# A two-layer attention and SwiGLU kernel: moving small SBUF tiles ahead of the large ones, with fillers

## The chip, the cores and the metric

The kernel runs on one core of a Trainium2 chip. The metric is device time in microseconds of one execution. The core has five engines that run their own instruction streams and wait for each other through semaphores: PE (matrix products), DVE (vector), ACT (activations), POOL (GpSimd) and SP, which here only issues DMAs. SBUF is the on-chip memory of 128 partitions from which PE reads both of its operands; PSUM is where PE writes.

## The reference

Two identical rounds of attention with one key and value head (16 query heads of 28, 2048 tokens, width 448), each followed by a SwiGLU feed-forward of width 1792, all in float32.

```python
def _A_ref(x, wq, wk, wv, wo):
    q = (x @ wq).reshape(B, S, H, Dh).transpose(0, 2, 1, 3)
    k = x @ wk
    v = x @ wv
    scores = jnp.einsum("bhqd,bkd->bhqk", q, k) * (Dh ** -0.5)
    p = _softmax(scores, axis=-1)
    o = jnp.einsum("bhqk,bkd->bhqd", p, v)
    return o.transpose(0, 2, 1, 3).reshape(B, S, H * Dh) @ wo

def _B_ref(x, w_gate, w_up, w_down):
    return (_silu(x @ w_gate) * (x @ w_up)) @ w_down

x = x + _A_ref(_layernorm(x), ...)   # and
x = x + _B_ref(_layernorm(x), ...)   # both twice
```

## The kernel before

**Precision.** Most products are made of three matmuls in the type float32r, which takes one column of the moving operand per clock: each operand is split into a rounded high part and the rest (`xh` and `xl`, `wgh` and `wgl`, `wdh` and `wdl`, `woh` and `wol`, `onh` and `onl`; the two halves of `keys`, of `qstack` and of `h2`), and high × high, high × low and low × high are summed in PSUM. Only P·V is in plain float32, which the compiler runs as two halves per matmul.

**Stages.** The rows of x stay in SBUF as `xres`, 16 tiles of 128 rows by 448. A layer first projects queries, keys and values (function `product_T`, L315, 512 columns per matmul), and sends the queries through DRAM into three buffers `qstack0` to `qstack2`, which stand for 16 steps of four heads. Attention then runs 128 cycles per layer (`cycle`, two key tiles each). One cycle computes scores for two key tiles, 2 × 12 matmuls at L643: four heads lie in four strips of 32 partitions, so four matmuls run side by side, and three such steps make up the precise product. ACT takes the exponent of three heads from PSUM (L669, tile `pt`), DVE copies the fourth head to SBUF (L666, tile `pair`) and ACT takes its exponent there (L671). P·V of the cycle before (L703) follows the scores on PE. At certain cycles the output projection with `wo` is put in (`half_rows`, L631 and `full_rows`, L622).

The feed-forward takes 14 blocks of 128 hidden columns in groups of two, and four blocks of 512 rows each; one such unit is 42 matmuls of 512 columns for gate and up and 24 of 448 columns for the down product. They are written out by `side_by_side` (L335) in two lists, one for the lower 64 partitions and one for the upper 64, that run next to each other. ACT, DVE and POOL form silu(g) · u, split it (`h2`, whose low half DVE writes at L1041) and add the down product to `xres`. A few units run on the whole array (`product_T` again, and `by_tile`, L898).

**Order.** Every engine's order is the order in which the code is written (`manual_schedule`); the code places work into cycles by tables of numbers. Tiles come from pools. A pool places a tile, when it is first asked for, behind the tiles that it has, each rounded up to 32 bytes; a name that is asked for again goes to one of its `bufs` places, in turn. Pools lie behind one another; `ow` fills from the other end of SBUF. So where a tile starts follows from the order and the sizes of what was asked for before it. With `reuse_waits="tile"` a tile waits for the earlier tiles on whose bytes it lies.

The pool `pers` begins at a multiple of 256 bytes (`xres` is its first tile). The small tiles after `xres` shift everything behind it. These are the starts of the tiles that PE reads, in bytes past a multiple of 256:

| tiles | before | after |
|---|---|---|
| `xres` (read by DVE and POOL) | 0 | 0 |
| `keys`, `vsb`, `ident`, `xn` | 32 | 0 |
| `qstack`, `xh`, `xl`, `xd`, `wh`, `wl`, `wgh`, `wgl`, `wdh`, `wdl`, `pt`, `pair`, `q2` | 64 | 0 |
| `h2`, `woh`, `wol`, `onh`, `onl` | 224 | 0 |
| `kdiag` | 192 | 0 |

Rows inside these tiles are 512, 1792 or 2048 bytes long, all multiples of 256 (of `vsb` 128), so every slice that a matmul reads starts at the same offset as its tile (in `vsb` also 128 more).

The program also holds a second, slower version of the whole computation (`full` is true), which is entered only where a check on the softmax sums fails; it isn't executed here.

Of the kernel before, what the change touches and what calls it, by code (L numbers as in the profile page):

```python
# [8 lines left out]
F32 = mybir.dt.float32  # L9
F32R = mybir.dt.float32r  # L10
# [5 lines left out]
P = 128  # L16
S = 2048
D = 448
# [4 lines left out]
NT = S // P  # L23
# [13 lines left out]
@with_exitstack  # L37
def kernel(ctx: ExitStack, tc: tile.TileContext, *aps):

    nc = tc.nc
    keep = ctx.enter_context(tc.tile_pool(name="keep", bufs=1))
    fine = keep.tile([P, 16], F32, name="fine")
    nc.gpsimd.memset(fine, 1.0)
    least = keep.tile([P, 1], F32, name="least")
    whole = keep.tile([1, 1], F32, name="whole")
    forward(tc, (fine, least, whole), False, *aps)
    ok = nc.values_load(whole[0:1, 0:1].bitcast(mybir.dt.int32), skip_runtime_bounds_check_because="compared with 0 only")  # L50
    with tc.If(ok == 0, label="again"):
        forward(tc, None, True, *aps)
# [3 lines left out]
def forward(  # L56
# [24 lines left out]
    pers = ctx.enter_context(tc.tile_pool(name="pers", bufs=1))  # L81
# [52 lines left out]
    def split(hi, lo, raw):  # L134
        nc.gpsimd.tensor_scalar(hi, raw, 1.0, 0.0, ALU.mult, ALU.add)
        nc.gpsimd.tensor_tensor(lo, raw, hi, ALU.subtract)

    xres = pers.tile([P, NT, D], F32, name="xres")
    stats = pers.tile([P, NT, 6], F32, name="stats")
    mv = pers.tile([P, NT, 2], F32, name="mv")  # L140
    halfn = pers.tile([P, 4], F32, name="halfn")
    ident = pers.tile([P, P], F32, name="ident")
    vsb = pers.tile([P, NT, 32], F32, name="vsb")
    keys = [pers.tile([P, 2, 512], F32R, name=f"keys{c}") for c in range(NC)]
    warm = pers.tile([P, 1], F32, name="warm")
    qts = [pers.tile([P, 2, 512], F32R, name=f"qstack{n}") for n in range(3)]
    qraw = pers.tile([P, 512], F32, name="qraw")
    bottom = pers.tile([4, 32], F32, name="bottom")
    kd, mask = None, None
    if not full:  # L150
        kd, mask = pers.tile([P, 4, P], F32R, name="kdiag"), pers.tile([P, 16, 4], F32, name="mask")

    def weights(fc):
        fs = slice(P * fc, P * fc + P)
# [175 lines left out]
    def side_by_side(lower, upper):  # L330

        assert len(lower) == len(upper)
        for two in zip(lower, upper):
            for po, (a, b), start, stop in two:
                nc.tensor.matmul(po, a, b, start=start, stop=stop, skip_group_check=True)  # L335

    seen = pers.tile([P, 4], F32, name="seen")

    def between(*pos):

# [5 lines left out]
    class Attention:  # L346
# [229 lines left out]
        def scores(self, ff, xb):  # L576
            next(switch)
            inner = ExitStack()
            with tc.tile_pool(name=f"ow{self.layer}", bufs=1, side="right", reuse_waits="tile") as ow:
# [72 lines left out]
                bufs = [wp.tile([P, 3, 512], F32, name=f"pt{y}") for y in range(4)]  # L652
# [66 lines left out]
                def post(i):  # L719

                    c, g = GR[i]
                    out2 = accs.pop(i)
                    oraw, rb = out2[:, 0, :], out2[:, 1, :]
                    rs = ow.tile([P, 16], F32, name="rs", bufs=2)
                    nc.sync.dma_start(rs, oraw[DH::32, :].rearrange("j (p n) -> j p n", n=16))

                    def rest():
                        if fine is not None:
                            under = ow.tile([P, 16], F32, name="under", bufs=2)
                            for bound, op in ((LIMIT, ALU.is_lt), (1.0 / LIMIT, ALU.is_gt)):  # L730
                                nc.vector.tensor_scalar(under, rs, bound, None, op)
                                nc.vector.tensor_tensor(fine, fine, under, ALU.mult)
                        nc.vector.reciprocal(rs, rs)
                        rd = dram.tile([4, 512], F32, name="rd", bufs=2)
                        nc.sync.dma_start(rd.rearrange("j (p n) -> (j p) n", n=16), rs)
                        nc.sync.dma_start(rb, rd[:, None, :].to_broadcast([4, 32, 512]))
                        if g == 0:
                            on[c] = (
                                ow.tile([P, NG, 512], F32R, name="onh"),
                                ow.tile([P, NG, 512], F32R, name="onl"),  # L740
                            )
                        nc.gpsimd.tensor_tensor(rb, oraw, rb, ALU.mult)

                    def spread():
                        if g == 0:
                            moved[c] = dram.tile([2 * DH, 512], F32, name=f"moved{self.layer}_{c}")
                            for q in (0, 1):
                                nc.sync.dma_start(moved[c][DH * q : DH * q + DH, :], rb[64 + 32 * q : 64 + 32 * q + DH, :])
                            for q in (0, 1):
                                n0 = 2 * DH - 8 + 4 * q  # L750
                                nc.sync.dma_start(rb[32 * q + DH : 32 * q + 32, :], moved[c][n0 : n0 + 4, :])
                            nc.sync.dma_start(rb[64:128, :], rb[0:64, :])
                            return
                        n0 = 16 * g - 16
                        for q in range(4):
                            nc.sync.dma_start(rb[DH + q :: 32, :], moved[c][n0 + 4 * q : n0 + 4 * q + 4, :])

                    def parts():
                        oh, ol = on[c]
                        split(oh[:, g, :], ol[:, g, :], rb)  # L760
                        if g == NG - 1 and c < NC - 1:
                            todo.append(c)

                    return rest, spread, parts

                X0 = xtile(xpool)
# [441 lines left out]
```

## Time and profile before

| | us |
|---|---|
| median of 3 runs | 1944.67 (1944.64 to 1945.7) |
| the profiled execution | 1948.05 |
| its span | 1946.3 |
| PE busy | 1933.1 (99%) |
| ACT busy | 1256.8 (65%) |
| DVE busy | 978.1 (50%) |
| POOL busy | 563.8 (29%) |

How to read it. The rows of the page's part 5 name a line, an engine, an operation, the tile written and the tiles read, then the shape and the count; behind the bar stand the busy time in us, the mean duration of one in ns, and the idle time of the engine just before these instructions with what ended it. PEld is PE's weight load, which runs beside matmuls. A matmul's duration includes the way through the array, so matmuls overlap in the records, and a busy PE may still be slower than it could be. The pace, from the start of one matmul to the start of the next, is read from the timeline, whose rows begin with a start time in us and a duration in us, and merge neighbours of one kind (x3: three of them). Rows of a table of windows begin with the window and its length, then busy time and count for each engine, then the granted clock of PE, the share of the DMA engines and GB/s. Line numbers are those of the kernel before; in the kernel after, lines behind the top of `forward` are 11 higher.

### The profile page before, as it was taken

How to read it: one execution, taken by the hardware profiler on the slowest of the kernel's cores; microseconds unless marked ns; L12 is line 12 of the kernel's file. 1: busy time of each engine (PE TensorE's matmuls, PEld its weight loads, DVE VectorE, ACT ScalarE, POOL GpSimd, SP SyncE). 2: the span in 40 equal slices, each digit the busy share in tenths (PEclk: the TensorE clock that was granted, in tenths of full speed). 3: DMA queues.
4: the chain of work that ended last, by engine and by line, in shares of the span. 5: the costliest groups of instructions: out<-in, count | busy, mean ns of one | idle time of the engine just before them, and what ended most of it. 6: DMA issues, size and time to landing. Idle time of an engine off the chain costs nothing. (4 is left out here: it accounts for less than half of the span.)

```text
span 1946.3 us, 43775 instructions
## 1 busy us (share of the span) xinstructions
PE 1933.1 (99%) x18369; PEld 1325.7 (68%) x18369; DVE 978.1 (50%) x1675; ACT 1256.8 (65%) x1863; POOL 563.8 (29%) x608
## 2 busy tenths in 40 slices
PE   9999999999999999999999999999999999999998
PEld 7544544445469999999974445454454799988887
DVE  6655575665754322322665565657656532232223
ACT  4799899898953333333359998989989433333332
POOL 4213123122215333432342221122231352333420
PEclk9999999999999999999999999999999999999999
DMA  5211011021122011100251110110211220011102
GB/s 160 63 33 33 20 32 50 23 54 33 35 81 73 17 33 32 32 19 25 60 156 48 34 34 18 43 38 26 53 52 30 81 61 26 17 32 32 33 2 77
DMA packets 105474, 87.52 MB, mean 45 GB/s; under 512 B 25304, under 2 KB 85464, under 8 KB 105272
## 3 DMA queue, kind: packets, MB, share of 16 engines
q1 hardware_dynamic: 103576, 83.25, 15.4%
q8 instruction: 144, 2.36, 0.5%
q10 hardware_dynamic: 1696, 1.43, 0.2%
q14 instruction: 58, 0.48, 0.1%
HBM read 59.48 MB, written 23.33 MB: 43 GB/s over the span
## 5 line engine op out<-in xcount | busy, mean ns | idle before, releaser
L669 ACT ACTIVATE pt<-three 128x1536 f32<-128x1536 f32 x512 | 722.1, 1478 | 52.9 <-PE three L643 52.8
L703 PE MATMUL bank<-pt,vsb 128*32 128x512 f32 x3072 | 490.8, 598 | 0.6 <-ACT pt L669 0.6
L703 PE MATMUL bank<-pair,vsb 128*32 128x512 f32 x1024 | 487.7, 598 | 0.0
L643 PE MATMUL bank<-qstack,keys 32*128 32x512 f32 x1536 | 472.7, 425 | 0.0
L335 PE MATMUL bank<-xh,wgh 64*128 64x512 f32 x1712 | 439.0, 389 | 0.4 <-ACT seen L342 0.4
L643 PE MATMUL three<-qstack,keys 32*128 32x512 f32 x4608 | 429.0, 408 | 0.5 <-ACT stage L549 0.3
L643 PEld LDWEIGHTS bank<-qstack,keys 32*128 32x128 f32 x1536 | 243.2, 183 | 248.1 <-issue 125.4
L666 DVE COPY pair<-bank 128x512 f32<-128x512 f32 x512 | 353.9, 691 | 96.5 <-PE bank L643 65.6
L335 PE MATMUL bank<-xh,wgl 64*128 64x512 f32 x1391 | 363.8, 390 | 0.0
L335 PE MATMUL bank<-xl,wgh 64*128 64x512 f32 x1284 | 329.5, 389 | 0.0
L1035 DVE TENSOR_TENSOR sg<-bank,sg 128x512 f32<-128x512 f32 x112 | 77.3, 690 | 486.8 <-ACT sg L1034 476.3
L335 PE MATMUL bank<-wdh,h 64*128 64x448 f32 x1728 | 320.8, 363 | 0.8 <-DVE h L1041 0.4
L671 ACT ACTIVATE pair<-pair 128x1024 f32<-128x1024 f32 x254 | 277.6, 1093 | 0.0
L643 PEld LDWEIGHTS three<-qstack,keys 32*128 32x128 f32 x4608 | 262.0, 183 | 14.2 <-DVE xres L614 1.5
L703 PEld LDWEIGHTS bank<-pt,vsb 128*32 128x32 f32 x3072 | 101.7, 109 | 249.2 <-issue 153.2
L335 PEld LDWEIGHTS bank<-xh,wgh 64*128 64x128 f32 x1712 | 260.9, 184 | 15.2 <-issue 1.0
L915 POOL TENSOR_TENSOR xres<-stage,xres 128x448 f32<-128x448 f32 x107 | 126.1, 1197 | 479.9 <-ACT stage L914 479.7
L711 DVE TENSOR_TENSOR o<-bank,o 128x512 f32<-128x512 f32 x224 | 154.7, 691 | 202.1 <-PE bank L703 202.0
L335 PEld LDWEIGHTS bank<-wdh,h 64*128 64x128 f32 x1728 | 238.4, 184 | 12.4 <-DVE h L1041 1.2
L342 ACT COPY seen<-bank 128x1 f32<-128x1 f32 x646 | 79.4, 163 | 244.7 <-PE bank L335 242.0
L335 PEld LDWEIGHTS bank<-xh,wgl 64*128 64x128 f32 x1391 | 214.9, 184 | 12.6
L335 PE MATMUL bank<-wdl,h 64*128 64x448 f32 x864 | 212.0, 366 | 0.0
(150 smaller groups left out, 2133.2 us busy)
## 6 DMA issues: line engine op xcount, KB each, us to landing
o<-rd SPq DMA_DIRECT2D x32, 256.0 KB
qraw<-qd SPq DMA_DIRECT2D x128, 56.0 KB
xt<-tb SPq DMA_DIRECT2D x32, 224.0 KB
wdr<-in_B_w_down_dram SPq DMA_DIRECT2D x28, 224.0 KB
xn<-xt SPq DMA_DIRECT2D x8, 768.0 KB
wr<-in_B_w_gate_dram SPq DMA_DIRECT2D x28, 192.0 KB
wr<-in_B_w_up_dram SPq DMA_DIRECT2D x28, 192.0 KB
qd<-stage SPq DMA_DIRECT2D x20, 224.0 KB
```

The costliest lines, as they stand in the source:

```text
L335: nc.tensor.matmul(po, a, b, start=start, stop=stop, skip_group_check=True)
L342: nc.scalar.copy(seen[:, i : i + 1], po[:, 0:1])
L643: nc.tensor.matmul(three[:, j, :] if j < 3 else one, k[js, kp, ks], q[js, part, :], start=(z == 0), stop=(z == 2), tile_position=(32 * j, 0),)
L666: copies.append(nc.vector.tensor_copy(pt1, one))
L669: es.append(nc.scalar.activation(pt, threes[y], AF.Exp, scale=SCALE))
L671: es.append(nc.scalar.activation(pair, pair, AF.Exp, scale=SCALE))
L703: nc.tensor.matmul(to[32 * j : 32 * j + 32, :], vsb[:, n % NT, :], pts[n][j], start=(y == 0), stop=(y == 1), skip_group_check=True,)
L711: f = nc.vector.tensor_tensor(accs[i][:, 0, :], to, accs[i][:, 0, :], ALU.add)
L915: nc.gpsimd.tensor_tensor(r, s, r, ALU.add)
L1035: nc.vector.tensor_tensor(in_order(sg, True), natural(pg[1], True), in_order(sg, True), ALU.mult)
```

## The change

The small tiles of the pool `pers` are asked for first, also those that used to be asked for only when they were first needed (`rstd`, `few`, `ng`, `two`, `flat`, `seen`); a filler `pad` of 112 floats brings the next tile to a multiple of 256 bytes. `xres` and the large tiles follow. In the pool `ow` a filler of 120 floats is asked for behind the pair `onh`, `onl`. The result for the tiles' starts is in the table above. Nothing is written to a filler, and the early calls write nothing: the later calls of the same names get the same places.

```diff
-    xres = pers.tile([P, NT, D], F32, name="xres")
     stats = pers.tile([P, NT, 6], F32, name="stats")
     mv = pers.tile([P, NT, 2], F32, name="mv")
+    ident = pers.tile([P, P], F32, name="ident")
     halfn = pers.tile([P, 4], F32, name="halfn")
-    ident = pers.tile([P, P], F32, name="ident")
+    warm = pers.tile([P, 1], F32, name="warm")
+    bottom = pers.tile([4, 32], F32, name="bottom")
+    seen = pers.tile([P, 4], F32, name="seen")
+    mask = None
+    if not full:
+        mask = pers.tile([P, 16, 4], F32, name="mask")
+        for _ in range(2):
+            pers.tile([P, 4], F32, name="rstd", bufs=2)
+        pers.tile([P, 8], F32, name="few")
+        pers.tile([P, 64], F32, name="ng")
+        pers.tile([P, 4, 2, 16], F32R, name="two")
+        pers.tile([P, P], F32, name="flat")
+        pers.tile([P, 112], F32, name="pad")
+    xres = pers.tile([P, NT, D], F32, name="xres")
     vsb = pers.tile([P, NT, 32], F32, name="vsb")
     keys = [pers.tile([P, 2, 512], F32R, name=f"keys{c}") for c in range(NC)]
-    warm = pers.tile([P, 1], F32, name="warm")
     qts = [pers.tile([P, 2, 512], F32R, name=f"qstack{n}") for n in range(3)]
     qraw = pers.tile([P, 512], F32, name="qraw")
-    bottom = pers.tile([4, 32], F32, name="bottom")
-    kd, mask = None, None
+    kd = None
     if not full:
-        kd, mask = pers.tile([P, 4, P], F32R, name="kdiag"), pers.tile([P, 16, 4], F32, name="mask")
+        kd = pers.tile([P, 4, P], F32R, name="kdiag")
...
-
-    seen = pers.tile([P, 4], F32, name="seen")
...
                                 ow.tile([P, NG, 512], F32R, name="onh"),
                                 ow.tile([P, NG, 512], F32R, name="onl"),
                             )
+                            if not full:
+                                ow.tile([P, 120], F32, name="pad")
```

The order of instructions on PE, ACT, POOL and SP is the same before and after, row by row. On DVE the instructions stand in the same order too, with other waits at one place of each layer: at the first transposes into the tile `tb3` (shown as tb), in the first group of the feed-forward. Before, in a row:

```order
L230 TENSOR_SCALAR xn<-xres,mv,rstd 128x448 [waits DVE_49,Pool_49]
L271 STREAM_TRANSPOSE tb_6629<-xn 128x14x32 [waits DMAHW2_49,DVE_49]
L271 STREAM_TRANSPOSE tb_6629<-xn 128x14x32 [waits DVE_49] x3
L1035 TENSOR_TENSOR sg<-bank_6453,sg 128x512 [waits Activation_49]
L911 TENSOR_TENSOR xres<-bank_6455,xres 128x448 [waits PE_49]
```

After, in a row:

```order
L241 TENSOR_SCALAR xn<-xres,mv,rstd 128x448 [waits DVE_49,Pool_49]
L282 STREAM_TRANSPOSE tb_6640<-xn 128x14x32 [waits DVE_49] x4
L1046 TENSOR_TENSOR sg<-bank_6464,sg 128x512 [waits Activation_49]
L922 TENSOR_TENSOR xres<-bank_6466,xres 128x448 [waits PE_49]
L1052 TENSOR_TENSOR h_6745<-sg,h_6745 128x512 [waits DMAHW6_49,DMAHW5_49,DMAHW7_49,DMAHW0_49,Activation_49]
```

`tb3` lay over the bytes of the tile `rs` of attention before and waited for the last DMA on them (DMAHW2); now it lies behind them, and that wait stands at a later DVE instruction, the first copy into `xl`.

## The prediction

> **What bounds the kernel now.** I read the page first, then the distance from one matmul's start to the next in the timeline, because a PE that is busy 99% of the span says only that matmuls overlap without a hole, not that they follow each other as fast as they can.
>
> ```profile
> span 1946.3 us, 43775 instructions
> PE 1933.1 (99%) x18369; PEld 1325.7 (68%) x18369; DVE 978.1 (50%) x1675; ACT 1256.8 (65%) x1863; POOL 563.8 (29%) x608
> L703 PE MATMUL bank<-pt,vsb 128*32 128x512 f32 x3072 | 490.8, 598 | 0.6 <-ACT pt L669 0.6
> L643 PE MATMUL three<-qstack,keys 32*128 32x512 f32 x4608 | 429.0, 408 | 0.5 <-ACT stage L549 0.3
> L335 PE MATMUL bank<-xh,wgh 64*128 64x512 f32 x1712 | 439.0, 389 | 0.4 <-ACT seen L342 0.4
> L335 PE MATMUL bank<-wdh,h 64*128 64x448 f32 x1728 | 320.8, 363 | 0.8 <-DVE h L1041 0.4
> L335 PE MATMUL bank<-wdl,h 64*128 64x448 f32 x864 | 212.0, 366 | 0.0
> ```
>
> PE waits for nothing in any large group (idle before: 0.0 to 0.8 us each). So the time is the number of matmul steps times the pace of a step, and nothing on another engine, queue or DMA can save time as long as it hides behind PE. The diff issues the same instructions in the same order (below). Its whole effect on PE must therefore come through the pace. Here are the paces, in settled stretches of matmuls with one matmul to a step. The first fence is 512 columns at a granted clock of 0.50 (start of the kernel), then 512 columns at 1.00, first and last of 34.
>
> ```profile
> 14.70:17.80 3.10, 3.10 (x9) 2.37 (x8) 3.00 (x8) 0.00 (x0) 1.67 (x6) 0.50 1.03 397
> 562.10:569.60 7.50, 7.50 (x34) 6.20 (x33) 3.18 (x9) 1.81 (x3) 0.00 (x0) 1.00 0.25 65
> ...
> 14.75 0.63 PE L315 MATMUL bank<-xh,wh 128*128 128x512 f32 x1
> ...
> 17.74 0.63 PE L315 MATMUL bank<-xh,wl 128*128 128x512 f32 x1
> ...
> 562.13 0.39 PE L315 MATMUL bank<-xh,wgl 128*128 128x512 f32 x1
> ...
> 569.61 0.40 PE L315 MATMUL bank<-xh,wgl 128*128 128x512 f32 x1
> ```
>
> At half clock seven steps take 2.99 us, 427 ns each: 1.2 columns per ns. At full clock the stream alone should take half, 213.5 ns. It takes 7.48 us / 33 = 226.7 ns: 13.2 ns too much, which at half clock is not there at all. The next rows are 448 columns (stream alone 186.7 ns): 24 matmuls whose moving tile is `woh`, then 24 whose moving tile is `wdh` or `wdl`, first and last of each.
>
> ```profile
> 1174.19 0.37 PE L622 MATMUL three<-wol,onh 128*128 128x448 f32 x1
> ...
> 1178.85 0.36 PE L622 MATMUL three<-woh,onh 128*128 128x448 f32 x1
> ...
> 1936.14 0.37 PE L898 MATMUL bank<-wdh,h 128*128 128x448 f32 x1
> ...
> 1940.86 0.37 PE L898 MATMUL bank<-wdh,h 128*128 128x448 f32 x1
> ```
>
> 4.66/23 = 202.6 ns and 4.72/23 = 205.2 ns: 15.9 and 18.5 ns over the stream. The two have the same shape, the same weight tile offset (224) and differ in where the moving operand starts: 224 and 64 bytes past a multiple of 256. Finally P·V, whose fp32 matmuls run as two halves at two clocks per column.
>
> ```profile
> 251.13 0.60 PE L703 MATMUL bank<-pt,vsb 128*32 128x512 f32 x3
> ...
> 251.56 0.60 PE L703 MATMUL bank<-pt,vsb 128*32 128x512 f32 x3
> ...
> 251.99 0.60 PE L703 MATMUL bank<-pt,vsb 128*32 128x512 f32 x3
> ```
>
> 0.43 us a step against 2 × 213.5 = 427: an excess of about 3 ns or less, with its moving tile at offset 64 as well. So the excess appears only where columns are taken at the full rate of one float per 1/2.4 ns. Something that delivers the moving operand can't keep up by 13 to 18 ns a step there, and is hidden when the array takes half as much.
>
> My reading: delivery is in blocks of 128 bytes (32 columns, 32/2.4 = 13.3 ns). 2048 bytes from offset 64 touch 17 blocks instead of 16, and 17 × 13.3 = 226.7, the measured pace to the tenth. 1792 bytes from 64 or 224 touch 15 instead of 14, 200.0 ns, plus 2.6 or 5.2 that this doesn't explain. The block is an inference from these four numbers; no operand at a multiple of 128 is streamed at full rate anywhere in this trace.
>
> **The change part by part.** Instructions: none added, none removed. The unused tiles allocate without being written. On PE, ACT, POOL and SP every instruction keeps its place; DVE loses two wait-only entries, because `tb3` no longer lies over the old `rs` tiles. The wait for those tiles' last DMA goes to the first copy of `xl`. Its price is nothing: the last DMA out of `rs` is issued at 1525.9 and the last transposes into `tb3` (named tb here) run until 1550.5, some 25 us later; the DMA had landed.
>
> ```profile
> L735 SPq DMA_DIRECT2D rd<-rs x32: 327/347/469, 109.2 to 1525.9; - x32
> ...
> L271 DVE STREAM_TRANSPOSE tb<-xn x32: 602/634/643, 276.8 to 1550.5; 128x448 f32<-128x448 f32 x32
> ```
>
> Transfers: rows in SBUF now start at multiples of 256. They may get shorter; all but the first load of x and the weights are hidden behind PE, and `xres`, which the start waits for, lay at a multiple of 256 already. Zero. ACT, DVE and POOL operands: hidden behind PE except in attention, below. Zero.
>
> Steps outside the score matmuls. These rows are the matmul counts (the second column with an x belongs to the weight loads) of L315, L441, L335, L622, L631 and L898, in this order.
>
> ```profile
> 0.00:1947.00 1947.00, 112.95 (x462) 87.30 (x462) 1.00 0.16 45
> 0.00:1947.00 1947.00, 8.99 (x32) 5.89 (x32) 1.00 0.16 45
> 0.00:1947.00 1947.00, 786.17 (x7086) 730.78 (x7086) 1.00 0.16 45
> 0.00:1947.00 1947.00, 60.52 (x288) 53.46 (x288) 1.00 0.16 45
> 0.00:1947.00 1947.00, 11.94 (x96) 8.46 (x96) 1.00 0.16 45
> 0.00:1947.00 1947.00, 10.34 (x48) 9.01 (x48) 1.00 0.16 45
> ```
>
> L335 and L631 run two halves of the array side by side, two matmuls to a step. Of L335's 7086, 1728 + 864 have 448 columns: 1296 steps; the other 4494 have 512: 2247 steps. 512 columns: 2247 + 462 + 32 = 2741 steps. 448 columns from offset 64: 1296 + 48 = 1344; from offset 224: 288 + 48 = 336; together 1680.
>
> A 512-column step saves its extra block, but keeps what P·V pays over its stream, about 2.5 ns: 226.7 − 216.0 = 10.7. Bounds: at best 13.2 (nothing over the stream); at worst a loss, from the slowest steps seen, the first ones after a change of clock or shape, 18.57 to 19.73 in the next rows, 5 steps of 232 ns: −5. I take 10.7, since P·V is the nearest row of a stream without the excess. A 448-column step saves one block, 13.3; bounds 18.5 (the whole excess) and, for a loss, the same −5.
>
> ```profile
> 18.57 0.39 PE L315 MATMUL bank<-xl,wh 128*128 128x512 f32 x1
> ...
> 19.73 0.39 PE L315 MATMUL bank<-xh,wh 128*128 128x512 f32 x1
> ```
>
> 2741 × 10.7 = 29.3 us and 1680 × 13.3 = 22.4 us.
>
> The Trainium skill, "TensorE: Matmul & The Clock Gate", section "Back-to-back issue gap", gives N/2.4 + 2.5 ns for a warm matmul: 215.8 and 189.2. The P·V rows and the half-clock rows agree with that page, the full-rate rows miss it by 11 to 16 ns. By it the two terms would be 29.9 and 26.0, an estimate.
>
> In the feed-forward part the faster PE must not run into DVE's `h`: it ends at 605.88 and its first reader starts at 606.56, 0.68 us later, while the 21 steps of the unit around it save at most 0.23. No stall follows.
>
> ```profile
> 605.19 0.69 DVE L1041 TENSOR_TENSOR h<-sg,h 128x512 fp32r<-128x512 f32 x1 [0.16 <-ACT h L1038]
> 606.56 0.55 PE L335 MATMUL bank<-wdh,h 64*128 64x448 f32 x2
> ```
>
> Attention: six score steps a cycle, 256 cycles (6144/24). PE could save 6 × 10.7 = 64 ns a cycle. ACT allows less. A usual cycle, then the quickest:
>
> ```profile
> 249.95 2.80 ACT L669 ACTIVATE pt<-three 128x1536 f32<-128x1536 f32 x2
> 252.63 1.07 ACT L671 ACTIVATE pair<-pair 128x1024 f32<-128x1024 f32 x1
> 253.59 2.79 ACT L669 ACTIVATE pt<-three 128x1536 f32<-128x1536 f32 x2
> ...
> 224.57 2.79 ACT L669 ACTIVATE pt<-three 128x1536 f32<-128x1536 f32 x2
> 227.23 1.08 ACT L671 ACTIVATE pair<-pair 128x1024 f32<-128x1024 f32 x1
> 228.18 2.81 ACT L669 ACTIVATE pt<-three 128x1536 f32<-128x1536 f32 x2
> ```
>
> ACT's cycle is 3.64 us and consists of its own work end to end (2.68 to the pair, 0.96 after it); the quickest is 2.66 + 0.95 = 3.61. I take 3.61 for ACT's own limit, from which it sets the pace, and count 0.03 × 256 = 7.7 us; without that limit it would be 16.4.
>
> Sum: 29.3 + 22.4 + 7.7 = 59.4 us. The profiled execution took 1948.05 us with a span of 1946.3, 3.4 above the median of 1944.67; taken off the median the time is **1885 us**.
>
> **Rivals.**
>
> *Only part of the excess depends on the start (18%).* For it: the two 448-column rows. 64 bytes past a block cost 18.5, 32 bytes short of one cost 15.9, so a price by bytes of the first broken block (64 and 32) fits: 2.6 ns per 32 bytes. Then a start at 0 saves 5.3 ns a step: 4421 × 5.3 = 23.4, and 7.7 in attention (6 × 5.3 = 32 ns still reaches ACT's limit): 1914 us. Against it: 17 blocks fit the 512 columns exactly.
>
> *The excess is a fixed start-up of every full-rate stream (15%, no measurable change).* For it: any fixed cost also vanishes at half clock, and no aligned row refutes it. Only the difference between the two 448-column rows is then up for change: 1344 × 2.6 = 3.5 us at most, 1941 to 1945 us. Against it: a fixed cost would not be 13.2, 15.9 and 18.5. Beside it stands the Trainium skill, "SBUF — State Buffer", section "Door 1: The DMA port swizzle", which speaks of lines of 16 bytes; every tile before starts at a multiple of 32, so by that page nothing is misaligned and nothing changes. No run here shows a 16-byte line.
>
> *Equal starts collide (15%, slower).* After the change the moving stream, the next weights and ACT's writes all start at the same place of a 256-byte row; before, `keys` lay at 32 against `qstack` at 64, `h` at 224 against `wdh` at 64. If a weight load then holds up the stream in every step, the price is that of the unsettled steps, 5 ns: 4421 × 5 = 22 us, and 6 × 5 × 256 = 8 in attention: about 1975 us. It decides from 1 ns a step (0.2% of the time). Against it: `xh` and `wgh` share offset 64 already and show the plain 226.7, and the pair with equal offsets (224 and 224) is the quicker of the 448-column rows.
>
> **How the numbers follow.** The block reading has 52% and gives 1885. Its low end takes the whole excess off: 2741 × 13.2 + 1344 × 18.5 + 336 × 15.9 + 7.7 = 74 us, 1870. The upper end takes in the partial case and the unchanged one: 1946. Left out are the slower case (15%) and small tails. A measurement of this kernel tells 0.2% (4 us) from no change: its runs lie within 1.1 us. Faster by more: 52 + 18 = 70%; within: 15%; slower: 15%.
>
> **What would show it.** Right: L315's settled 512-column steps at 216 ns, 448-column ones at 189 to 193; P·V unchanged at 0.43 us; attention's cycle near 3.60 us with PE now waiting for ACT. Wrong: 226.7 again (fixed cost), some 221 (partial), or over 227 (collision). A cycle near 3.57 would say that ACT's limit was mine, not the chip's; a wait of PE for `h` or for weights would show cover gone that I counted on.

## The result and the profile after

The changed kernel takes 1937.50 us (median of 7 runs, 1936.91 to 1939.11) against 1944.67 us for the kernel before (7 runs, 1943.50 to 1945.70): a ratio of 0.9963 with a 95% interval of 0.9954 to 0.9972. It is faster, by 0.37% or 7.2 us, and not by the 59 us forecast.

The page after, its first lines and the groups that answer to those shown of before:

```profile
span 1935.7 us, 43773 instructions
PE 1923.0 (99%) x18369; PEld 1325.8 (68%) x18369; DVE 979.0 (51%) x1675; ACT 1254.1 (65%) x1863; POOL 563.4 (29%) x608
L712 PE MATMUL bank<-pt,vsb 128*32 128x512 f32 x3072 | 490.8, 598 | 0.6 <-ACT pt L678 0.6
L652 PE MATMUL three<-qstack,keys 32*128 32x512 f32 x4608 | 428.8, 408 | 0.5 <-ACT stage L558 0.3
L346 PE MATMUL bank<-xh,wgh 64*128 64x512 f32 x1712 | 419.7, 390 | 0.0
L346 PE MATMUL bank<-wdh,h 64*128 64x448 f32 x1728 | 313.2, 361 | 0.8 <-DVE h L1052 0.5
```

PE is still busy 99% of the span and still waits for nothing; score and P·V groups stand as they were, and only the feed-forward groups (L335 before, L346 now) shrank: 439.0 to 419.7 us and 320.8 to 313.2. By the starts of the first score matmul and the last P·V matmul of each layer, the span divides as follows (us):

| | start | attention 0 | feed-forward 0, projection 1 | attention 1 | feed-forward 1 |
|---|---|---|---|---|---|
| before | 65.9 | 493.2 | 468.1 | 493.4 | 425.5 |
| after | 63.6 | 492.6 | 464.4 | 492.8 | 422.2 |

The two feed-forward stretches give 7.0 us. The start holds the stretch at half clock, which differs from run to run (the whole start lasts 63.4 to 64.7 us in the profiles of the seven full kernels below, whatever the layout). The profiled execution of before lay 3.4 us above its median, that of after on it, so the 2.3 us of the start and the 1.2 us of attention in this table are not counted as the change's.

The pace, in the timeline after: 23 settled full-array steps of 512 columns, then two stretches of 35 matmuls with `woh` or `wol` as moving tile, then 24 with `wdh` or `wdl`, first and last of each:

```profile
561.64 0.39 PE L326 MATMUL bank<-xh,wgl 128*128 128x512 f32 x1
...
566.63 0.39 PE L326 MATMUL bank<-xh,wgl 128*128 128x512 f32 x1
...
1167.24 0.37 PE L631 MATMUL three<-wol,onh 128*128 128x448 f32 x1
...
1174.27 0.37 PE L631 MATMUL three<-woh,onl 128*128 128x448 f32 x1
...
1528.42 0.37 PE L631 MATMUL bank<-wol,onh 128*128 128x448 f32 x1
...
1535.31 0.37 PE L631 MATMUL bank<-woh,onl 128*128 128x448 f32 x1
...
1925.55 0.36 PE L909 MATMUL bank<-wdh,h 128*128 128x448 f32 x1
...
1930.21 0.37 PE L909 MATMUL bank<-wdh,h 128*128 128x448 f32 x1
```

512 columns: 4.99/22 = 226.8 ns, as before, though the moving tile now starts at a multiple of 256. 448 columns: 4.66/23 = 202.6 ns for `wdh` (205.2 before) and 7.03/34 = 206.8 in one stretch with `woh`, 6.89/34 = 202.6 in the other (202.6 before). The kernel has eight such stretches: before, all eight go at 202.5 to 202.8 ns; after, six do and two go at 206.7, with the same tiles. So not one of the three settled rows went where the forecast sent it, and `woh` shows two lasting paces in one layout.

Most matmuls stand in the two-lane part, which repeats a round of 33 steps: 11 of 512 columns, 6 of 448, 10 of 512, 6 of 448. Here is the same place of a round, five rounds apart, before and then after (the first `wdl` step of the shorter half):

```profile
701.63 0.54 PE L335 MATMUL bank<-wdl,h 64*128 64x448 f32 x2
...
738.09 0.54 PE L335 MATMUL bank<-wdl,h 64*128 64x448 f32 x2
```

```profile
701.31 0.50 PE L346 MATMUL bank<-wdl,h 64*128 64x448 f32 x2
...
737.44 0.50 PE L346 MATMUL bank<-wdl,h 64*128 64x448 f32 x2
```

36.46/5 = 7.292 us a round before, 36.13/5 = 7.226 after. The kernel has 2247/21 = 107 rounds, and 107 × 0.066 = 7.1 us: the whole gain. Counted over all matmul records of one lane, from one start to the next: a 448-column step followed by another takes 202.8 ns in place of 205.5 (1071 pairs, 2.9 us), the step from 512 to 448 columns 227.4 in place of 236.5 (214, 1.9 us), the step from 448 to 512 199.4 in place of 201.0 (209, 0.3 us), and 512 to 512 goes from 229.8 to 228.9 (2028, 1.8 us). What in the new layout did this was the question for the runs.

### The profile page after: what moved, and what is told of

The parts are those of the page before. It is cut to its first block, busy times and chain, and to the rows that moved or that the text cites. A ratio compares the mean times of both kernels' runs of the same rounds, so it can differ in the third digit from the quotient of the medians.

```text
span 1935.7 us, 43773 instructions
## 1 busy us (share of the span) xinstructions
PE 1923.0 (99%) x18369; PEld 1325.8 (68%) x18369; DVE 979.0 (51%) x1675; ACT 1254.1 (65%) x1863; POOL 563.4 (29%) x608
## 5 line engine op out<-in xcount | busy, mean ns | idle before, releaser
L678 ACT ACTIVATE pt<-three 128x1536 f32<-128x1536 f32 x512 | 733.4, 1523 | 52.5 <-PE three L652 52.5
L346 PE MATMUL bank<-xh,wgh 64*128 64x512 f32 x1712 | 419.7, 390 | 0.0
L346 PE MATMUL bank<-xh,wgl 64*128 64x512 f32 x1391 | 349.2, 388 | 0.0
L346 PE MATMUL bank<-wdh,h 64*128 64x448 f32 x1728 | 313.2, 361 | 0.8 <-DVE h L1052 0.5
L346 PE MATMUL bank<-xl,wgh 64*128 64x512 f32 x1284 | 312.4, 386 | 0.0
L680 ACT ACTIVATE pair<-pair 128x1024 f32<-128x1024 f32 x254 | 289.2, 1139 | 0.0
L346 PEld LDWEIGHTS bank<-xh,wgh 64*128 64x128 f32 x1712 | 241.6, 184 | 12.7 <-issue 1.0
L346 PEld LDWEIGHTS bank<-wdh,h 64*128 64x128 f32 x1728 | 225.2, 184 | 10.0 <-DVE h L1052 1.2
L346 PEld LDWEIGHTS bank<-xh,wgl 64*128 64x128 f32 x1391 | 200.8, 184 | 11.8
L1045 ACT ACTIVATE sg<-bank 128x512 f32<-128x512 f32 x112 | 66.9, 597 | 217.2 <-PE bank L346 212.9
```

The source lines that it names most:

```text
L678: es.append(nc.scalar.activation(pt, threes[y], AF.Exp, scale=SCALE))
L680: es.append(nc.scalar.activation(pair, pair, AF.Exp, scale=SCALE))
L1045: nc.scalar.activation(in_order(sg, True), natural(pg[0], True), AF.Silu)
```

## The experiments

The theories. *Block reading* (theory B, the forecast's own): the moving tile's start alone decides, in blocks of 128 bytes. *Multiples of 256* (theory A): the large tiles' own places count. *Fixed start-up* (theory F): neither. *Pairs* (called theory W, the weights' start, in the first series, and pair theory later): what counts is where the moving tile starts against the weight tile that is loaded while matmuls run; before, `h` as weights lay at 224 and `wdh` as moving tile at 64, and now both lie at 0.

### Series of matmuls with chosen starts

```diff
+        for i in range(32): mm(b[i % 4][:, 0:512], sta[:, 16 + 128 * (i % 4) : 144 + 128 * (i % 4)], mov[:, 0 + 512 * (i % 2) : 512 + 512 * (i % 2)], start=True, stop=True)  # N 512 mov 0 sta 64
...
```

> Leaves out the whole computation (the input is copied to the output) and runs series of 32 float32r matmuls, each series on a line of its own, with nothing to wait for; the moving tile's start, the weights' start and the number of columns change from series to series. Fixed start-up (theory F): the pace of 512 columns is 226 to 227 ns whatever the two starts are, of 448 columns 200 to 203 ns, and over all widths it is columns/2.4 ns plus a constant of 12 to 15 ns. Block reading (theory B, the one the forecast rests on): 213 to 216 ns at starts that are multiples of 128 bytes, 226 to 227 ns at the others, and the moving tile's start alone decides. Weights' start (theory W): 448 columns go at 202 to 203 ns where the weights start at the same offset from a multiple of 256 bytes as the moving tile or at 0, and at 205 to 206 ns where the weights start at 224 and the moving tile at 64, as it was in the kernel before; 512 columns do not change.

The timeline of PE has one row a series; the distance between two rows' starts, divided by 32, is the pace. Each series is shown with the row behind it: 512 columns with moving/weights starts 0/0 (L30) and 0/64 (L39); 448 columns with 0/0 (L48), 64/64 (L49), 224/224 (L50), 64/224 (L51), 0/224 (L52) and 64/0 (L53):

```profile
30.93 7.42 PE L30 MATMUL bank<-mov,sta 128*128 128x512 f32 x32
38.19 7.57 PE L31 MATMUL bank<-mov,sta 128*128 128x512 f32 x32
...
97.72 7.63 PE L39 MATMUL bank<-mov,sta 128*128 128x512 f32 x32
105.18 7.65 PE L40 MATMUL bank<-mov,sta 128*128 128x512 f32 x32
...
164.15 6.65 PE L48 MATMUL bank<-mov,sta 128*128 128x448 f32 x32
170.64 6.65 PE L49 MATMUL bank<-mov,sta 128*128 128x448 f32 x32
177.13 6.76 PE L50 MATMUL bank<-mov,sta 128*128 128x448 f32 x32
183.72 6.73 PE L51 MATMUL bank<-mov,sta 128*128 128x448 f32 x32
190.29 6.70 PE L52 MATMUL bank<-mov,sta 128*128 128x448 f32 x32
196.83 6.56 PE L53 MATMUL bank<-mov,sta 128*128 128x448 f32 x32
203.23 6.64 PE L54 MATMUL bank<-mov,sta 128*128 128x448 f32 x32
```

0/0 goes at 7.26/32 = 226.9 ns, 0/64 at 233.1, and by the same view 64/64 at 227.5 (the first steps after a change included). An aligned moving tile is no quicker than one at 64, so the block reading is out; and moving the *weights* by 64 bytes costs 6 ns, so a fixed start-up isn't all either. 448 columns: 202.8 at 0/0 and at 64/64, but 205.9 at 224/224; 205.3 at 64/224, which are the starts and the pace of the kernel before; 204.4 at 0/224; and 200.0 at 64/0, better than with equal starts. Over widths, equal starts give columns/2.4 + 13.3 ns at 320, 384 and 512 (146.7, 173.3 and 226.7 once settled), and up to 3.4 ns more between 416 and 496. So there is a fixed part of 13.3 ns, as theory F says, and a part on top of it, 0 to 7 ns, that depends on the two starts. Theory W's values came out at 0/0, 64/64 and 64/224. They missed 224/224, where the starts are equal, and 64/0 and 32/0 (205.9), where the weights lie at 0; its sentence that 512 columns do not change was wrong too.

### One group of tiles alone, and the change without it

The kernel before with the tiles of `halves` (h2, o2 and the query weights' parts) moved, all others where they were:

```diff
@@ before
+    if not full:
+        pers.tile([P, 24], F32, name="gap")
...
+                if not full:
+                    pers.tile([P, 40], F32, name="gap_")
```

> The kernel before with fillers ahead of and behind one group of tiles alone: h2, o2 and the query weights' halves start at 64 in place of 224 from a multiple of 256 bytes, as their moving tiles wdh and wdl do; all other large tiles stay as they were (none of those at 64 or 32 is at a multiple of 128). Theory W (the weights' start, alone or against the moving tile's) gives the whole gain of the change: 1937.5 to 1938.5 us, the two-lane 448-column steps at 202.8 ns in place of 205.5. Theory A (it needs multiples of 256 bytes for the moving tiles): 1944 to 1945 us, 205.5 ns.

The changed kernel with only this group back at 224 (the front filler is shortened by 256 bytes, since the room is needed):

```diff
@@ after
-        pers.tile([P, 112], F32, name="pad")
+        pers.tile([P, 48], F32, name="pad")
...
+    if not full:
+        pers.tile([P, 56], F32, name="gap")
...
+                if not full:
+                    pers.tile([P, 8], F32, name="gap_")
```

> The changed kernel with h2, o2 and the query weights' halves put back to a start of 224; all other large tiles are at multiples of 256 bytes. Theory W gives the gain back: 1943.5 to 1945 us, the two-lane 448-column steps at 205 to 206 ns. Theory A (moving tiles at multiples of 256 bytes are what counts): 1937 to 1938.5 us, 202.8 ns.

The changed kernel with everything 64 bytes further on:

```diff
@@ after
-        pers.tile([P, 112], F32, name="pad")
+        pers.tile([P, 128], F32, name="pad")
...
-                                ow.tile([P, 120], F32, name="pad")
+                                ow.tile([P, 104], F32, name="pad")
```

> The changed kernel with every large tile moved by 64 bytes: all starts are equal and none is a multiple of 128. Theory W in its relative form (equal starts suffice): 1937 to 1938.5 us, as the changed kernel. Theory A and theory B (multiples of 256 or of 128 count for themselves): 1943 to 1945 us.

Each run next to its own runs of the kernel before; the round is read from the timeline as above:

| kernel | starts of x, wg, wd, h | median us | ratio, 95% interval | round us |
|---|---|---|---|---|
| before | 64, 64, 64, 224 | 1944.67 | | 7.292 |
| after | 0, 0, 0, 0 | 1937.50 | 0.9963 [0.9954, 0.9972] | 7.226 |
| h alone | 64, 64, 64, 64 | 1938.46 | 0.9968 [0.9956, 0.9980] | 7.226 |
| all at 64 | 64, 64, 64, 64 | 1938.13 | 0.9970 [0.9960, 0.9980] | 7.226 |
| h back at 224 | 0, 0, 0, 224 | 1947.94 | 1.0016 [1.0007, 1.0025] | 7.332 |

One group moved by 96 bytes, with hardly a tile at a multiple of 128 or 256, has the round of the whole change and a time that its interval does not tell from it. The whole change without this group loses to the kernel before. And all tiles at 64 do as well as all at 0. Theory A and the block reading are out on all three; what the change gains is the distance between `h` and `wdh`. The expectation for h back at 224 was too low by 3 us: it took the gain back and 3 us more. Its rows, in the timeline, five rounds apart:

```profile
700.13 0.56 PE L351 MATMUL bank<-wdl,h 64*128 64x448 f32 x2
...
736.79 0.56 PE L351 MATMUL bank<-wdl,h 64*128 64x448 f32 x2
```

36.66/5 = 7.332. Counted modulo 256 bytes, the moving tile starts 32 bytes past its weights here (0 against 224) and 96 past in the kernel before (64 against 224): the two distances have their own prices.

### The two-lane order, the next step's weights, and the fixed part

```diff
+        def alt(n, *starts):
+            for i in range(48):
+                m, s = starts[i % len(starts)]
+                yield b[i % 4][:, 0:n], sta[:, s // 4 + 128 * (i % 4) :][:, 0:128], mov[:, m // 4 + 512 * (i % 2) :][:, 0:n]
...
+        def lanes(xm, xs, dm, ds):
+            for r in range(3):
+                for u in (11, 10):
+                    for i in range(u + 6):
+                        for lane in (0, 64):
...
+        for z in lanes(0, 0, 0, 192): mm(*z, start=True, stop=True)  # lanes(0, 0, 0, 192)
```

> Leaves out the whole computation, as the first series did. Three questions. (1) Which two starts have to agree? Series of 512 columns whose steps alternate between moving/weights starts 32/0 and 0/32 (each step's own two differ, its moving tile and the next step's weights agree), and between 32/32 and 0/0 (the reverse). If a stream meets the load of the next step's weights, the first goes at 226.7 to 227.5 ns and the second at 231 to 235; if a step's own two tiles count, it is the other way round. (2) What are the 13.3 ns that stay at the best starts (226.7 ns for 512 columns, 200.0 for 448 with the moving tile 64 bytes ahead)? With 96, 64 and 32 weight columns in place of 128: if the load of the weights takes this time from the stream, 223, 220 and 217 ns; if it is a start-up of the stream, 226.7 for all. (3) Which starts suit the feed-forward part's two-lane order (11 steps of 512 columns, 6 of 448, 10 of 512, 6 of 448)? The kernel before (64, 64, 64, 224) is to come out slowest by 2.7 ns for each 448-column step, and the 448-column moving tile 64 bytes ahead of its weights is to gain another 2.8 ns for each.

The timeline of PE, where each round shows as two rows with `mov` (its 22 and its 20 matmuls of 512 columns). Start of the second round and of the series behind the third, two rounds apart: all starts 0 (L79), h at 192 (L82), the starts of the kernel before (L95):

```profile
304.67 2.68 PE L79 MATMUL bank<-mov,sta 64*128 64x512 f32 x22
...
319.12 2.68 PE L80 MATMUL bank<-mov,sta 64*128 64x512 f32 x22
...
369.82 2.65 PE L82 MATMUL bank<-mov,sta 64*128 64x512 f32 x22
...
384.14 2.66 PE L83 MATMUL bank<-mov,sta 64*128 64x512 f32 x22
...
652.22 2.69 PE L95 MATMUL bank<-mov,sta 64*128 64x512 f32 x22
...
666.81 2.69 PE L96 MATMUL bank<-mov,sta 64*128 64x512 f32 x22
```

7.225, 7.160 and 7.295 us a round. With nothing to wait for and without ACT or DVE at work, the series give the rounds of the kernels to within 0.003 us: 7.292 before, 7.226 after; and 7.333 for h at 224 alone, 7.332 in the kernel. Of the 26 combinations tried the best is h at 192 with everything else at 0, and 7.160 is 21 × 226.7 + 12 × 200.0 ns: nothing but the stream and the fixed part. Within a round the starts do three things. They set the pace of the 448-column steps, and they set how the next 512-column steps begin: with equal starts these come at 236, 228, 232, 231 and then 227 ns, with h at 192 at 227 from the first. And they set the last 512-column step ahead of the 448-column ones, although its own two tiles have equal starts in the kernels compared: it takes 237 ns in the kernel before, behind steps that had settled at 227, then 227 in the changed kernel and 235 with `h` alone back at 224 (medians). So the next step's weights count too.

Question (1) stays open: with steps alternating between starts 32/0 and 0/32, and between 32/32 and 0/0, both series go at 231.6 ns, between the 226.7 of equal starts and the 233.3 of unequal ones. Neither the step's own pair nor the pair with the next step's weights carries it alone. The same with 96 and with 64 bytes points opposite ways: 230.4 against 234.2 ns, for the next step's weights, and 232.9 against 231.9, for the step's own. Question (2): 512 columns with 128 and with 32 weight columns (L71, L74), each with the row behind it; 96 and 64 weight columns lie between:

```profile
241.89 7.45 PE L71 MATMUL bank<-mov,sta 128*128 128x512 f32 x32
249.18 7.53 PE L72 MATMUL bank<-mov,sta 128*96 128x512 f32 x32
...
263.90 7.57 PE L74 MATMUL bank<-mov,sta 128*32 128x512 f32 x32
271.31 6.58 PE L75 MATMUL bank<-mov,sta 128*128 128x448 f32 x32
```

227.8 and 231.6 ns, and 230.0 for 96 and for 64: fewer weight columns make a step no quicker, so the load of the weights doesn't take the 13.3 ns column by column. Nor was it 226.7 for all, as a start-up alone would give. So a start-up of the stream is what is left of the two, and not shown; what it consists of, no run shows.

### The prediction of the series, tried in the kernel

```diff
@@ after, h2, o2 and the halves at 192
-        pers.tile([P, 112], F32, name="pad")
+        pers.tile([P, 48], F32, name="pad")
...
+    if not full:
+        pers.tile([P, 48], F32, name="gap")
...
+                if not full:
+                    pers.tile([P, 16], F32, name="gap_")
```

> The changed kernel with h2, o2 and the query weights' halves at 192 from a multiple of 256 bytes, everything else at 0: the 448-column stream starts 64 bytes after its weights. Pair theory (the two starts of a step against each other set the pace; the two-lane series tell by how much): a round of 33 steps takes 7.160 us in that series against 7.227 us with all starts equal, and the feed-forward part has 107 rounds, so 7.2 us less than the changed kernel: 1930 to 1931 us, 448-column steps at 200.0 ns, 512-column steps at 226.7. Theory of multiples of 256 (the changed kernel is the best there is): 1943 to 1948 us, as with 224.

The same with the two gaps exchanged (16 and 48):

> The same with h2, o2 and the halves at 64. Pair theory, by the series (7.187 us a round): 4.3 us less than the changed kernel, 1933 to 1934 us. Theory of multiples of 256: 1943 to 1948 us.

And the moving tiles shifted in place of the weights:

```diff
@@ after, with the pad at 48
+        if not full:
+            wpool.tile([P, 16], F32, name="gap")
         dh = wpool.tile([P, D], F32R, name="wdh", bufs=FG + 1)
         dl = wpool.tile([P, D], F32R, name="wdl", bufs=FG + 1)
+        if not full:
+            wpool.tile([P, 48], F32, name="gap_")
```

> The changed kernel with wdh and wdl at 64 in place of moving h: the same 64 bytes between a 448-column step's two starts as with h at 192, but other distances to the 512-column steps ahead and behind. Pair theory in its simple form (only the step's own two starts count): 1933 to 1934 us from 448-column steps at 200 ns. By the series (7.227 us a round, since the 512-column steps behind need five steps to come down to 226.7): no gain, 1937 to 1938.5 us.

Last, the kernel before with fillers of 8 and 120 floats at the two places of the diff for h alone:

> The kernel before with h2, o2 and the halves alone moved, from 224 to 0 from a multiple of 256 bytes; wdh, wdl, xh and wgh stay at 64, the rest at 32, 192 and 224. The 448-column stream starts 64 bytes after its weights, as with h at 192 in the changed kernel. Pair theory, by the series (7.160 us a round against 7.293 in the kernel before): 14.3 us less than before, 1930 to 1931 us, though hardly a tile lies at a multiple of 256 bytes. Theory of multiples of 256: 1944 to 1945 us.

| kernel | starts of x, wg, wd, h | median us | ratio, 95% interval | round us | series |
|---|---|---|---|---|---|
| after, h at 192 | 0, 0, 0, 192 | 1931.61 | 0.9931 [0.9917, 0.9945] | 7.160 | 7.160 |
| after, h at 64 | 0, 0, 0, 64 | 1935.06 | 0.9951 [0.9937, 0.9965] | 7.186 | 7.187 |
| after, wd at 64 | 0, 0, 64, 0 | 1936.82 | 0.9961 [0.9947, 0.9975] | 7.228 | 7.227 |
| before, h at 0 | 64, 64, 64, 0 | 1934.31 | 0.9948 [0.9934, 0.9962] | 7.160 | 7.160 |

No series has the starts 64, 64, 64, 0; the last row names that of 0, 0, 0, 192, whose distances are the same.

The timeline of h at 192, then of wd at 64, five rounds apart:

```profile
701.19 0.43 PE L351 MATMUL bank<-wdl,h 64*128 64x448 f32 x2
...
736.99 0.43 PE L351 MATMUL bank<-wdl,h 64*128 64x448 f32 x2
```

```profile
701.02 0.53 PE L350 MATMUL bank<-wdl,h 64*128 64x448 f32 x2
...
737.16 0.53 PE L350 MATMUL bank<-wdl,h 64*128 64x448 f32 x2
```

35.80/5 = 7.160 and 36.14/5 = 7.228: the series forecast every round to 0.001 us. The times lie 0.6 us (h at 192) and 1.1 us (h at 64) above what was expected, and 0.2 us (wd at 64) below. With h at 192 the kernel's 448-column steps take 200.0 ns and its 512-column steps 226.9 on the mean of a lane: both at the stream plus 13.3 ns, the least that any start tried gave. This kernel beats both others, by 5.9 us the changed one. wd at 64 has the same 64 bytes within each 448-column step and gains nothing, as the series said and the simple pair theory didn't: its 512-column steps take 229.3 ns on the mean, since each group begins with 231, 236, 228, 232 and 231, and its 448-column steps 201.8. The kernel before with its `h` moved to 0 reaches the same round as the best, and its time is 3 us beside the expectation: its two attention stages take 493.8 and 493.9 us against 492.7 and 492.8 with h at 192. Which tile does that wasn't tried.

### Pace against distance

```diff
+        def far(n, d, base=0):
+            for i in range(32):
+                yield b[i % 4][:, 0:n], sta[:, 320 + base // 4 : 448 + base // 4], mov[:, 256 + (base + d) // 4 :][:, 0:n]
```

> Leaves out the whole computation, as the first two series did: 32 matmuls a line with one fixed moving tile and one fixed weight tile, whose distance grows by 64 bytes from line to line, for 512 and for 448 columns; then some distances again with both tiles moved on by 64 and by 192. Pair theory: the pace depends on the distance and repeats, every 256 bytes if the row of 256 bytes is what counts, or every 512 if the difference between the first two series (202.8 and 206.7 ns for 448 columns with both starts at multiples of 256, where the tiles lay 0 and 256 bytes apart modulo 512) is due to the distance; moving both tiles on changes nothing. 512 columns: 226.7 ns at the best distances and up to 234 elsewhere; 448 columns: 200.0 at 64 to 207. If the absolute start counts as well, the last lines differ from the first at equal distance.

Rows of the timeline: 512 columns at distances 0, 64, 128 and 192 (L34 to L37), then 448 columns at 0 and 64 (L51, L52) and at 256 and 320 (L55, L56), with the row behind each group:

```profile
33.22 7.42 PE L34 MATMUL bank<-mov,sta 128*128 128x512 f32 x32
40.47 7.50 PE L35 MATMUL bank<-mov,sta 128*128 128x512 f32 x32
47.81 7.59 PE L36 MATMUL bank<-mov,sta 128*128 128x512 f32 x32
55.24 7.62 PE L37 MATMUL bank<-mov,sta 128*128 128x512 f32 x32
62.70 7.44 PE L38 MATMUL bank<-mov,sta 128*128 128x512 f32 x32
...
158.49 6.65 PE L51 MATMUL bank<-mov,sta 128*128 128x448 f32 x32
164.98 6.57 PE L52 MATMUL bank<-mov,sta 128*128 128x448 f32 x32
171.39 6.68 PE L53 MATMUL bank<-mov,sta 128*128 128x448 f32 x32
...
184.38 6.77 PE L55 MATMUL bank<-mov,sta 128*128 128x448 f32 x32
190.99 6.56 PE L56 MATMUL bank<-mov,sta 128*128 128x448 f32 x32
197.39 6.69 PE L57 MATMUL bank<-mov,sta 128*128 128x448 f32 x32
```

Settled, 512 columns take 226.7, 229.0, 232.3 and 233.3 ns at distances of 0, 64, 128 and 192, and the same four again for each further 256 up to 1024. 448 columns take 202.5, 199.9, 203.7 and 202.3, then 206.7, 200.0, 204.0 and 202.0 from 256 on, and this repeats each 512. With both tiles moved on by 64 or 192 the paces return within 0.4 ns, but for one: 448 columns at distance 0, moved on by 192, go at 206.7 in place of 202.5. So the distance decides, nearly alone. Some distances have two lasting paces, and which of them a series falls into isn't set by the distance: the stretches with `woh` above went at 202.6 and 206.8 ns in one kernel, and 512 columns at 64 bytes go at 229.0 here and in the first series, but at 233.3 in the alternating series after another predecessor.

## Why the prediction was wrong

**The bound.** Right: PE's steps are the time, no wait appeared, and the change could only act through the pace.

**The excess of 13.2 ns as one extra block.** This is the step that failed. "17 × 13.3 = 226.7, the measured pace to the tenth" was one number fitted by one free block size, and so no evidence: with aligned tiles, which touch no extra block, the pace is 226.8 in the kernel and 226.7 in the series. The term of 2741 × 10.7 = 29.3 us measured 0 in settled full-array steps and 3.7 us in the two-lane part (512 to 512 and 512 to 448), for another reason. The rival of a fixed start-up had this part right: 13.3 ns stay at the best distances tried for 448 and 512 columns. That the time fell at all, as forecast, is luck: the block had no part in it.

**The 448-column rows, 205.2 against 202.6.** The prediction saw that the two had the same weight offset and looked at the moving tile's offset alone. It was the distance of the two tiles: 0 with `woh` and `onh` (224 and 224), 96 bytes with `wdh` and `h` (64 and 224, modulo 256). The forecast even noted, against its rival of equal starts, that the pair with equal offsets was the quicker, and didn't price it. The term of 22.4 us measured 3.2 us for the two-lane steps (448 to 448 and 448 to 512); the full-array `woh` rows, with equal starts before and after, gained nothing, and two of their eight stretches went from 202.7 to 206.7.

**Attention, 7.7 us.** Measured 1.2 us for both layers, and nothing in the pace of either kind of matmul. Even the 1.2 us are not shown to be the layout's: h alone, whose score and P·V tiles lie as before, takes 492.9 us in each layer. The score matmuls changed their distance from 32 to 0, where settled series would gain 6.6 ns a step. In the kernel they come six steps at a time and don't settle: behind the first, a step takes 230 to 235 ns before and 230 to 241 after (medians). ACT's cycle after, four cycles apart:

```profile
243.77 2.82 ACT L678 ACTIVATE pt<-three 128x1536 f32<-128x1536 f32 x2
...
258.27 2.82 ACT L678 ACTIVATE pt<-three 128x1536 f32<-128x1536 f32 x2
```

14.50/4 = 3.63 us, against 3.64 before. Since PE's score steps did not get quicker, whether ACT limits at 3.61 was not put to the test.

**What was costed at nothing.** Transfers, DVE's `h` and the moved waits cost nothing, as forecast: the only waits ahead of the L346 groups in the page are 0.8 us.

**The rivals.** Fixed start-up was nearest, with 1941 to 1945 us. Its floor was right and its sum too small: it counted 1344 × 2.6 = 3.5 us, and left out that the starts of one group also change the step into it (9.1 ns × 214) and how the next group begins (0.9 ns × 2028). Equal starts collide: the price of 5 ns was of the right size, the sign was wrong for 512 columns. For 512 columns equal starts are the best (226.7 ns settled), and unequal ones cost 2.3 to 6.6 ns; for 448 columns equal starts do cost 2.5 to 6.7 ns over a moving tile 64 bytes ahead.

**The two rules beside it.** The Trainium skill, "TensorE: Matmul & The Clock Gate", section "Back-to-back issue gap", gives N/2.4 + 2.5 ns as the gap of an isolated warm matmul, and the forecast held a stream of them against it. Here streams of float32r matmuls measure N/2.4 + 13.3 at their best (146.7, 173.3 and 226.7 ns at 320, 384 and 512 columns), and 111.6 ns for 64 and 128 columns alike. The Trainium skill, "SBUF — State Buffer", section "Door 1: The DMA port swizzle", speaks of lines of 16 bytes. Taking alignment to these lines as all that counts, the forecast expected no change beside its rival, since all tiles start at multiples of 32. The measurement differs: 64 bytes between two tiles are worth up to 6.7 ns a step, so these lines don't account for what the matmuls showed.

## What to carry to other kernels

Where PE is busy without a hole in float32r matmuls, compare the time between matmul starts with columns/2.4 ns plus 13.3: what is above it may come from the distance of the moving tile from the weight tile, and a filler of a few floats ahead of one group of tiles may remove it, as it did here. Alignment as such bought nothing here; one group moved did all that the rearranged layout did, and the same group 64 bytes lower (192 in place of 256) nearly doubled it, 7.2 to 13.1 us. A series of bare matmuls in the kernel's own order forecast the kernel's round to 0.003 us, so such a layout is better measured than reasoned out, and a fit of one number by one unknown is no evidence.

## What the runs showed of the hardware that was not expected

- With float32r operands a matmul's pace depends on the distance between its moving and its weight tile in SBUF: 226.7 to 233.3 ns for 512 columns (period 256 bytes), 199.9 to 206.7 ns for 448 columns (period 512 bytes), with both tiles in one place throughout a series.
- The effect has a memory. After a change of shape 512-column steps come at 236, 228, 232 and 231 ns before they settle at 226.7, and some distances have two lasting paces (202.5 and 206.7 ns; 229.0 and 233.3 ns).
- A weight load takes some 0.19 us and runs under the stream ahead of it, so the two are under way at the same time. In the timeline of the kernel after, the load for the step with `wgl` begins 0.01 us after the matmul ahead of it:

```profile
562.09 0.39 PE L326 MATMUL bank<-xl,wgh 128*128 128x512 f32 x1
562.10 0.19 PEld L326 LDWEIGHTS bank<-xh,wgl 128*128 128x128 f32 x1
```

That load and stream get in each other's way there would explain the distance, and that the next step's weights change a step (227 against 237 ns). It is argued, not shown: the alternating series don't lean one way, and what makes the periods and the two lasting paces stays open.
